# Loads of the norm weights on another queue, and the first q and k transposes of the second batch in another PSUM bank

## The chip, the cores and the metric

The kernel runs on one core of a Trainium2 chip. Five engines work from instruction streams of their own[...]: TensorE (PE, matmuls and their weight loads, PEld), VectorE (DVE), ScalarE (ACT), GpSimd (POOL) and SyncE (SP, which here only issues DMAs). The metric is the device time of one execution in microseconds (us); lower is better.

## The reference

Two stages follow each other. The first is attention over 8 batches, 12 heads, 448 positions and a head size of 64, with q and k normalised by their root mean square:

```python
q_n = q / sqrt(mean(q*q) + 1e-6) * g_q          # the same for k with g_k
scores = softmax(q_n @ k_n.T / sqrt(64))
attn = scores @ v
```

The second takes the heads side by side as x (3584 rows, 768 columns) and applies `h = x @ w_in` (2048 columns), `g = h * clip(h + 3, 0, 6) / 6`, `out = g @ w_out`. Inputs and output are float32 in HBM.

## The kernel before, in words

**Tiling.** The unit of attention is a pair of heads, P = 0 to 47, six pairs to a batch. A pair passes through five functions:

- `loads` brings k, q and v of the pair in three DMAs of 224 KB. All are issued by SP, except that q of the first three pairs is issued by ACT. Buffers for k and q are five deep.
- `prep` squares q and k (line 320 on ACT for the first three pairs, lines 322 and 329 on DVE or POOL for the others), sums the squares per head and row (DVE, line 337), turns the sums into 1/rms (two ACT instructions, lines 343 and 344), multiplies (line 351, `qks`, DVE or POOL), and casts v (POOL, line 359, `va`).
- `turn` transposes k and q so that the head size lies on the partitions. For P below `NPE` = 10, that is the whole first batch (P 0 to 5) and four pairs of the second (P 6 to 9), PE does it: eight transposes of 112x112 (line 377) into one PSUM bank, then two copies by DVE out of the bank, `kp` (line 381, multiplied by `gp`) and `kq` (line 383). From P = 10 on a DMA transpose does it (line 388), and `kp` is made by POOL or DVE (line 392).
- `attend` makes the scores (PE, line 416, into the two-bank buffers S) and their exponentials (ACT, line 421), four tiles to a pair.
- `gather` multiplies by v (PE, line 437) into the bank X (positions 0 to 383) and the bank R (the last 64), and DVE normalises out of X (lines 462 and 463, `xn`). For the first batch PE transposes `xn` into an M bank (line 476) and DVE copies it to `xT` (line 480); later batches use DMA transposes (line 486).

`gp`, one value per partition, is 8 * g_q * g_k. It is made once by DVE (line 270) from four loads of 64 values each (`load_g`, lines 254 and 255): g_q and g_k, each once for the upper and once for the lower 64 partitions.

The MLP of a batch follows one batch later: `h_group` (line 533, six matmuls into an M bank, then ACT line 539 and DVE line 541 out of it) sixteen times, and `y_group` (line 558, sixteen matmuls into an M bank, then DVE line 566). Its matmuls are spread between the attention of the next batch. The weights w_in and w_out come through eight DMAs of POOL's queue (lines 277 and 283), held back by a small copy on POOL (line 621, `mark`) until q of the third pair has landed.

**PSUM.** There are eight banks: two S buffers of two banks each, X with one, R with one, and M with two. Each is a `Ring`: a taker waits until everyone who used the buffer before it is done. In the kernel before, the M ring serves `turn` (P 0 to 9), the `xn` transposes of the first batch, `h_group` and `y_group`, in the order in which these are called. X serves `gather` alone.

**Order.** Each piece of work is a `Step` with the engines that may take it, an expected duration, a due time and the steps it depends on. `Plan.order` is a list scheduler over these: it walks through time, gives each engine the ready step that is due first, and so fixes the order on every engine and, where a step may go to DVE or POOL, the engine. The program then issues in that order; on the chip each engine keeps to it. A changed duration, engine or dependency can therefore reorder work anywhere behind it. The loads of SP and ACT take eight completion semaphores in turn, and a load waits on its own queue until the earlier load with the same semaphore has landed. The loads of POOL have eight of their own.

Of the kernel before, what the change touches and what calls it, by code (L numbers as in the profile page):

```python
# [33 lines left out]
class Plan:  # L34
# [12 lines left out]
    def add(self, on, dur, due, fn, *deps, xfer=0.0, after=0.0, lock=False, late=0.0):  # L47
        on, f = ({on: dur}, lambda e: fn()) if isinstance(on, str) else (on, fn)
        s = Step(on, due, f, deps, xfer, after, lock, late, len(self.steps))
        self.steps.append(s)  # L50
        return s
# [93 lines left out]
def kernel(  # L145
# [11 lines left out]
    nc = tc.nc  # L157
# [3 lines left out]
    NJ = H // 2  # L161
# [14 lines left out]
    def tiles(name, n, shape, dt=BF16, pool=const):  # L176
        return [pool.tile(shape, dt, name=f"{name}{i}") for i in range(n)]

    gq_t, gk_t, gp = (const.tile([128, 1], FP32, name=n) for n in ("gq_t", "gk_t", "gp"))
# [23 lines left out]
    X_r = Ring(tiles("X", 1, [128, 512], FP32, psum))  # L203
    R_r = Ring(tiles("R", 1, [128, 512], FP32, psum))
    M_r = Ring(tiles("M", 2, [128, 512], FP32, psum))

    plan = Plan()
    add = plan.add
# [42 lines left out]

    def load_g():
        for a in range(2):
            nc.scalar.dma_start(out=gq_t[a * 64:(a + 1) * 64, :], in_=g_q.rearrange("(p o) -> p o", o=1))
            nc.scalar.dma_start(out=gk_t[a * 64:(a + 1) * 64, :], in_=g_k.rearrange("(p o) -> p o", o=1))

    def make_ident():
        nc.gpsimd.memset(ident[:], 0.0)
# [4 lines left out]
    def make_ones():  # L263
        for t in va_r.bufs:
            nc.gpsimd.memset(t[:, :, :, D:E1], 1.0)
        for t in kp_r.bufs:
            nc.gpsimd.memset(t[:, S:S + 16], 0.0)

    g_load = add("ACT", 2.2, 0, load_g, after=1.5, late=3.0)
    g_make = add("DVE", 0.1, 0, lambda: nc.vector.scalar_tensor_tensor(  # L270
        out=gp[:], in0=gq_t[:], scalar=8.0, in1=gk_t[:], op0=MULT, op1=MULT), g_load, after=7.5)
    id_make = add("POOL", 0.5, 0, make_ident)
# [92 lines left out]
    def turn(P):  # L365
        at = begin[P]
        qks, qks_use, sc, va, va_use, vc = SC.pop(P)
        kq, war, kq_use = kq_r.take()
        kp, kwar, kp_use = kp_r.take()
        if P < NPE:  # L370
            m, mwar, m_use = M_r.take()
            pt = m[:].bitcast(BF16)[:, 0:2 * S].rearrange("p (i c) -> p i c", i=2)
            tr = []
            for i in range(2):
                def trans(i=i):
                    for t in range(T):
                        nc.tensor.transpose(  # L377
                            out=pt[:, i, t * PT:(t + 1) * PT],
                            in_=qks[0:PT, i, t].rearrange("p h d -> p (h d)"), identity=ident[0:PT, 0:PT])
                tr.append(add("PE", 0.4, at - 2, trans, sc[i], id_make, *mwar))  # L380
            ks = add("DVE", 0.45, at - 1, lambda: nc.vector.tensor_scalar_mul(  # L381
                kp[:, 0:S], pt[:, 0], gp[:, 0:1]), tr[0], g_make, one_make, *kwar)
            qc = add("DVE", 0.45, at - 1, lambda: nc.vector.tensor_copy(out=kq[:, 1], in_=pt[:, 1]), tr[1], *war)
            m_use += [ks, qc]
            qks_use += tr
            KQ[P] = (kq, kp, va, kq_use, kp_use, va_use, [ks, qc], vc)
        else:
            tr = add("SP", 1.3, at - 8, lambda: nc.sync.dma_start_transpose(
                out=kq[:].rearrange("p i (t c) -> p (i t) c", c=PT),
                in_=qks[0:PT].rearrange("p i t h d -> p (i t h d)")), *sc, *war, xfer=1.3, late=1.5)  # L390
            ks = add({"DVE": 0.34, "POOL": 0.6}, 0, at - 1, lambda e: (
                nc.vector if e == "DVE" else nc.gpsimd).tensor_scalar_mul(  # L392
                    kp[:, 0:S], kq[:, 0], gp[:, 0:1]), tr, g_make, one_make, *kwar, lock=True)
            qks_use.append(tr)
            kq_use.append(ks)
            KQ[P] = (kq, kp, va, kq_use, kp_use, va_use, [ks], vc)
# [232 lines left out]
    for P in range(NP):  # L629
        for fn, at in ((loads, -26), (prep, -13), (turn, -2), (attend, 0)):  # L630
            blocks.append((begin[P] + at, lambda fn=fn, P=P: fn(P)))
        blocks.append((begin[P + 1] + 0.1, lambda P=P: gather(P)))
# [41 lines left out]
```

## Time and profile before

| what | us |
|---|---|
| median of 4 runs | 441.49 (440.89 to 443.41) |
| the profiled execution, its own time | 440.89 |
| its span, first to last instruction | 439.1 |
| PE busy in the span | 410.4 |
| DVE, ACT, POOL busy | 245.0, 249.0, 240.5 |

The span is 1.8 us shorter than the time of the same execution. PE busy counts the stretches in which at least one matmul is in flight. Lines with a q after the engine (ACTq, SPq) are its sequencer, which issues DMAs and waits. The release named behind an idle stretch is the semaphore that came last. The clock that TensorE was granted is full in every slice.

### The profile page before, as it was taken

To read this page: it belongs to the slowest core of one execution; us is meant where nothing else is said; L and a number is where in the kernel's file an instruction comes from. 1 tells how busy PE (TensorE), PEld (TensorE's weight loads), DVE (VectorE), ACT (ScalarE), POOL (GpSimd) and SP (SyncE) were. 2 spreads that over 40 slices of the span, in tenths; PEclk is the share of its full clock that TensorE was granted. 3 is DMA by queue.
4 is the path that set the end of the run, shared out by engine and by line. 5 is a ranking of instruction groups with operands and counts; after the bars stand their busy time and mean duration, and the time that the engine had idled before them with its cause. 6 is when DMAs were issued, how large, how long until landed. Compare 5 with 4: busy or idle time off the path is not lost.

```text
span 439.1 us, 9205 instructions
## 1 busy us (share of the span) xinstructions
PE 410.4 (93%) x3663; PEld 229.1 (52%) x3682; DVE 245.0 (56%) x417; ACT 249.0 (57%) x425; POOL 240.5 (55%) x230
## 2 busy tenths in 40 slices
PE   0598799999999999999999999999999999999995
PEld 0255455555455555554455555554455555654563
DVE  1998887557674564456455465556564444334421
ACT  2688588657765666367664677357673665123200
POOL 3499988865757567656765657747757510000000
PEclk9999999999999999999999999999999999999999
DMA  9999999897455646674466655684466420220122
GB/s 232 258 269 261 221 216 196 206 185 204 113 136 141 186 116 138 162 214 116 128 156 163 171 138 149 159 210 113 116 162 168 97 56 11 64 72 0 37 72 73
DMA packets 102923, 64.58 MB, mean 147 GB/s; under 512 B 59744, under 2 KB 99424, under 8 KB 102880
## 3 DMA queue, kind: packets, MB, share of 16 engines
q1 hardware_dynamic: 94544, 57.01, 51.1%
q0 software_dynamic: 7296, 6.29, 9.2%
q10 hardware_dynamic: 1040, 0.69, 0.6%
q8 instruction: 29, 0.48, 0.4%
q14 instruction: 14, 0.11, 0.1%
HBM read 45.61 MB, written 11.01 MB: 129 GB/s over the span
## 4 chain that ended last, share of the span: by engine, by line
PE 82%; POOL 5%; DVE 3%; DMA 3%; issue 3%; ACT 2%; SPq 1%; POOLq 0%; DVEq 0%
PE M L558 27%; PE M L533 26%; PE S L416 9%; PE X L437 8%; PE S L558 4%; PE R L437 2%; PE S L533 2%; DMA qk<-in_k_dram 1%; POOL qks L351 1%; PE X L558 1%; DVE ssq L337 1%; POOL va L359 1%; POOL sq L322 1%; ACT e L421 1%; POOL sq L329 1%
## 5 line engine op out<-in xcount | busy, mean ns | idle before, releaser
L421 ACT ACTIVATE e<-S 112x896 bf16<-112x896 f32 x192 | 166.4, 914 | 64.1 <-PE S L416 64.1
L533 PE MATMUL M<-xT,w_in_sb 128*128 128x384 bf16 (+1 forms) x679 | 145.1, 349 | 3.8 <-DVE gT L541 3.0
L351 POOL TENSOR_TENSOR qks<-qk,rs 112x512 bf16<-112x512 f32 x87 | 90.6, 1057 | 85.9 <-ACT rs L344 84.0
L558 PE MATMUL M<-w_out_sb,gT 128*128 128x384 bf16 x736 | 131.8, 326 | 0.0
L558 PEld LDWEIGHTS <-gT 128*128 128x128 bf16 x896 | 82.9, 98 | 57.9 <-issue 7.8
L533 PEld LDWEIGHTS <-w_in_sb 128*128 128x128 bf16 x768 | 69.6, 97 | 67.5 <-issue 12.6
L541 DVE SCALAR_TENSOR_TENSOR gT<-t,M 128x384 bf16<-128x384 f32 (+1 forms) x116 | 70.7, 612 | 59.2 <-ACT t L539 58.5
L539 ACT ACTIVATE t<-M 128x384 f32<-128x384 f32 (+1 forms) x116 | 62.7, 540 | 66.8 <-PE M L533 65.3
L437 PEld LDWEIGHTS <-e 112*128 112x128 bf16 x1536 | 65.0, 99 | 31.4 <-issue 16.0
L337 DVE TENSOR_REDUCE ssq<-sq 112x16 f32<-112x1024 f32 (+1 forms) x49 | 58.4, 1193 | 25.3 <-POOL sq L329 14.0
L329 POOL TENSOR_TENSOR sq<-qk 112x1024 f32<-112x1024 f32 x36 | 68.3, 1896 | 0.0
L416 PE MATMUL S<-kq,kp 64*128 64x448 bf16 x384 | 56.6, 364 | 4.0 <-DVE kp L381 1.7
L437 PE MATMUL X<-va,e 112*128 112x65 bf16 x1152 | 58.5, 195 | 0.8 <-ACT e L421 0.6
L566 DVE COPY y<-M 128x384 f32<-128x384 f32 x46 | 25.6, 556 | 59.4 <-PE M L558 59.2
L359 POOL CAST va<-vf 112x512 bf16<-112x512 f32 x48 | 31.5, 658 | 10.2 <-DMA vf<-in_v_dram 9.3
L392 POOL TENSOR_SCALAR kp<-kq,gp 128x448 bf16<-128x448 bf16 x23 | 32.3, 1405 | 5.8 <-DMA kq<-qks 5.8
L463 DVE TENSOR_TENSOR xn<-X,rd 128x384 bf16<-128x384 f32 x48 | 26.8, 558 | 1.6
L416 PEld LDWEIGHTS <-kp 64*128 64x128 bf16 x384 | 12.2, 94 | 27.6 <-issue 18.8
L377 PE MATMUL M<-ident,qks 112*128 112x112 bf16 x80 | 8.0, 242 | 13.6 <-DVE qks L351 13.0
L437 PE MATMUL R<-va,e 112*128 112x65 bf16 x384 | 20.4, 195 | 0.0
L558 PE MATMUL S<-w_out_sb,gT 128*128 128x384 bf16 x112 | 19.5, 326 | 0.0
L462 DVE RECIPROCAL rd<-X 128x6 f32<-128x6 f32 x48 | 9.2, 192 | 14.7 <-PE X L437 14.6
(42 smaller groups left out, 155.0 us busy)
## 6 DMA issues: line engine op xcount, KB each, us to landing
qk<-in_k_dram SPq DMA_DIRECT2D x48, 224.0 KB, 3.2
vf<-in_v_dram SPq DMA_DIRECT2D x48, 224.0 KB, 3.9
qk<-in_q_dram SPq DMA_DIRECT2D x45, 224.0 KB, 3.5
w_in_sb<-in_moe_w_in_dram POOLq DMA_DIRECT2D x4, 768.0 KB, 10.4
w_out_sb<-in_moe_w_out_dram POOLq DMA_DIRECT2D x4, 768.0 KB, 10.7
out_dram<-y SPq DMA_DIRECT2D x8, 336.0 KB, 3.1
out_dram<-y SPq DMA_DIRECT2D x8, 288.0 KB, 3.6
out_dram<-y SPq DMA_DIRECT2D x8, 240.0 KB, 3.5
```

Source lines behind the costliest of these rows:

```text
L329: parts = [add("POOL", 1.93, at - 10, lambda: nc.gpsimd.tensor_tensor(out=sq[0:PT], in0=qk[0:PT], in1=qk[0:PT], op=MULT), *ld, *war, lock= ...
L337: red = add("DVE", 0.6 * n, at - 8 * hurry + 0.5 * i0, lambda i0=i0, i1=i1, cs=cs: nc.vector.tensor_reduce(out=ssq[0:PT, cs], in_=sq[0:PT, ...
L351: sc.append(add(on, 0, at - 6 * hurry, lambda e, i=i, rs4=rs4: engines[e].tensor_tensor(out=qks[0:PT, i].rearrange("p t h d -> p h t d"), ...
L359: vc = add({"POOL": 0.61}, 0, at - 3, lambda e: engines[e].tensor_copy(out=va[0:PT, :, :, 0:D], in_=vf[0:PT].rearrange("p h (t d) -> p h t ...
L392: nc.vector if e == "DVE" else nc.gpsimd).tensor_scalar_mul(
L416: nc.tensor.matmul(out=ps[:, a, 0:S], lhsT=kp[rows, c0:c0 + 128], rhs=kq[rows, 1, :], start=True, stop=True)
L421: x = add("ACT", 0.93, at + step * (t0 + i) / T + 0.2, lambda t=t0 + i, ps=ps: nc.scalar.activation(out=e[0:PT, t], in_=ps[0:PT, :, 0:S], ...
L437: nc.tensor.matmul(out=dst[:, a * E1:(a + 1) * E1], lhsT=e[0:PT, t, a, c0:c0 + 128], rhs=va[0:PT, a, t, :], start=(first and a == 0 and t ...
L533: nc.tensor.matmul(out=m[:, 0:n], lhsT=w_in_sb[:, kt, f * 128:(f + 1) * 128], rhs=X[:, kt, :], start=(kt == 0), stop=(kt == NKT - 1))
L539: r = add("ACT", 0.08 + n / 1200, due + span, lambda: nc.scalar.activation(out=t[:, 0:n], in_=m[:, 0:n], func=RELU, bias=0.5, scale=1.0 / ...
L541: g = add("DVE", 0.12 + n / 960, due + span, lambda: nc.vector.scalar_tensor_tensor(out=G[:, f, :], in0=t[:, 0:n], scalar=1.0, in1=m[:, 0: ...
L558: nc.tensor.matmul(out=m[:, 0:HALF], lhsT=G[:, f, i * 128:(i + 1) * 128], rhs=w_out_sb[:, f, cols], start=(f == 0), stop=(f == NFT - 1))
```

## The change

Two edits. The four loads of `load_g` are issued by POOL and no longer by ACT, with another entry for the planner: 2.5 on POOL, due at 1, in place of 2.2 on ACT, due at 0 and not before 1.5. And `turn` takes its bank from the M ring only for the first batch (`NJ` = 6); for P 6 to 9 it takes X.

```diff
     def load_g():
         for a in range(2):
-            nc.scalar.dma_start(out=gq_t[a * 64:(a + 1) * 64, :], in_=g_q.rearrange("(p o) -> p o", o=1))
-            nc.scalar.dma_start(out=gk_t[a * 64:(a + 1) * 64, :], in_=g_k.rearrange("(p o) -> p o", o=1))
+            nc.gpsimd.dma_start(out=gq_t[a * 64:(a + 1) * 64, :], in_=g_q.rearrange("(p o) -> p o", o=1))
+            nc.gpsimd.dma_start(out=gk_t[a * 64:(a + 1) * 64, :], in_=g_k.rearrange("(p o) -> p o", o=1))
...
-    g_load = add("ACT", 2.2, 0, load_g, after=1.5, late=3.0)
+    g_load = add("POOL", 2.5, 1, load_g, late=3.0)
...
         if P < NPE:
-            m, mwar, m_use = M_r.take()
+            m, mwar, m_use = (M_r if P < NJ else X_r).take()
```

In the order that results, POOL issues the four loads after its memsets and before `mark`; on DVE `gp` stands behind both `qks` of the first pair; five squares more go to DVE and five fewer to POOL, three `qks` go from DVE to POOL, and two `kp` of the later pairs go from POOL to DVE.

## The prediction

> **What bounds the kernel now.** I read the busy table first, then the sums by stage, then the order of time at the start, the chain, and PE's order of time where the second batch begins. From the page:
>
> ```profile
> span 439.1 us, 9205 instructions
> PE 410.4 (93%) x3663; PEld 229.1 (52%) x3682; DVE 245.0 (56%) x417; ACT 249.0 (57%) x425; POOL 240.5 (55%) x230
> ```
>
> PE is idle for 28.7 us of the span. Where that lies is in the sums by stretch (busy time of PE, PEld, DVE, ACT, POOL, then clock, DMA share and GB/s):
>
> ```profile
> 0.00:9.00 9.00, 0.00 (x0) 0.00 (x0) 0.00 (x0) 1.30 (x2) 2.26 (x17) 1.00 0.86 227
> 9.00:15.00 6.00, 1.35 (x10) 0.86 (x12) 4.81 (x9) 4.34 (x12) 1.97 (x3) 1.00 1.14 227
> 15.00:25.00 10.00, 7.78 (x67) 3.99 (x63) 9.96 (x13) 7.02 (x12) 6.78 (x8) 1.00 1.16 271
> ...
> 35.00:46.00 11.00, 8.43 (x125) 5.15 (x125) 9.77 (x20) 8.61 (x15) 10.99 (x12) 1.00 1.16 260
> 46.00:60.00 14.00, 11.99 (x136) 7.66 (x135) 11.85 (x20) 9.52 (x21) 13.46 (x16) 1.00 1.23 216
> 60.00:75.00 15.00, 14.85 (x150) 8.17 (x148) 11.37 (x23) 12.96 (x24) 13.67 (x12) 1.00 1.14 194
> 75.00:376.00 301.00, 298.84 (x2709) 165.27 (x2724) 167.40 (x284) 186.72 (x314) 182.17 (x158) 1.00 0.57 145
> ```
>
> From 75 us on PE is the bound: 2.2 us idle in 301. Whatever brings PE sooner to that stage, with the same work done, comes off the end. Before it there are three stages: a start without PE work (to about 12 us), the first batch (to 46), where DVE and then POOL are nearly full, and the first MLP groups (to 60), where PE stalls for 2 us. In the order of time the start reads:
>
> ```profile
> 4.18 0.53 ACTq L254 DMA_DIRECT2D gq_t<-in_g_q_dram  x1
> 4.75 0.60 ACTq L255 DMA_DIRECT2D gk_t<-in_g_k_dram  x1
> ...
> 7.12 0.47 ACTq L254 DMA_DIRECT2D gq_t<-in_g_q_dram  x1
> ...
> 8.47 0.47 ACTq L255 DMA_DIRECT2D gk_t<-in_g_k_dram  x1
> 8.99 1.67 ACT L320 ACTIVATE sq<-qk 112x512 f32<-112x512 f32 x3 [6.98 <-DMA gq_t<-in_g_q_dram]
> ...
> 12.16 0.16 DVE L270 SCALAR_TENSOR_TENSOR gp<-gq_t,gk_t 128x1 f32<-128x1 f32 x1 [0.44 <-DMA gk_t<-in_g_k_dram]
> ```
>
> The first square starts at 8.99, though its data are there long before: the first k load is issued at 0.73 and takes 3.4 us to land (4.16), the first q 3.8 from 0.76 (4.55). ACT does not come to it, because each of its four g loads waits for an earlier load with the same completion semaphore: they go out when the first k, the first q, v of pair 0 and k of pair 2 have landed. The squares stand behind. The chain confirms it: it is the longest piece of the first 12 us, followed by a g load that holds DVE until 12.16.
>
> ```profile
> 2.17 6.28 DMA qk<-in_k_dram
> 8.47 3.56 DMA gk_t<-in_g_k_dram
> ```
>
> Where the second batch begins, PE's order of time shows the M banks (line 533 is an MLP group, 377 a turn):
>
> ```profile
> 45.99 2.12 PE L533 MATMUL M<-xT,w_in_sb 128*128 128x384 bf16 x12
> ...
> 49.68 1.14 PE L533 MATMUL M<-xT,w_in_sb 128*128 128x384 bf16 x6 [0.53 <-DVE gT L541]
> 50.65 0.56 PE L377 MATMUL M<-ident,qks 112*128 112x112 bf16 x8
> 52.21 1.14 PE L533 MATMUL M<-xT,w_in_sb 128*128 128x384 bf16 x6 [1.00 <-DVE gT L541]
> ```
>
> The turn takes the second M bank, so two MLP groups follow each other in one bank, and the second waits 1.00 us until DVE has emptied it. With a third wait of 0.47 at 56.85, PE waits 2.0 us there for line 541.
>
> [...] ACT is idle for 6.98 us with its data landed. [...] The gain here isn't bandwidth but the place in ACT's queue. [...]
>
> **The change part by part.**
>
> *ACT without the g loads.* The first square (q is first in the new order) starts at 4.57 in place of 8.99: 4.42 us. The pieces behind it: before, the two 1/rms values end at 11.42, 2.43 after the first square's start. In the new order a square of pair 1's q (landed 5.95, 0.61 long) precedes the first of them, so they run from 6.58, four at some 0.2 with gaps, to 7.44. DVE's two `qks` (0.69 each) end at about 8.4, `gp` takes 0.16, the reduction for pair 1 1.2, and `kp` starts at about 9.7 in place of 13.97. Start: 4.3 us earlier.
>
> *POOL with the g loads.* POOL is idle from 1.6 to 7.75. The nearest row is the issue of w_in, 0.89 to 1.05 each with far more rows; four such are 4.2 us, done by 5.9 and covered by that idle time. [...] Landing: ACT's g loads took 3.6 to 5.5 us[...]. [...] DVE comes to `gp` at 8.4, so the cost is 0 to 3.0; I take 0, since on POOL's queue the g loads stand behind nothing, while on ACT's they stood behind three 224 KB loads. Nothing else waits for them: `mark` waits for a q load until 7.7 anyway, and w_in goes out 0.5 us sooner.
>
> *The first batch behind it.* DVE has no idle time to speak of from 12 to 46 us. To the last `xT` copy the new order gives it three squares more (2.1), four `qks` fewer (2.8) and one reduction earlier (1.2): 0.5 later. POOL loses most of its idle 4.0 and 3.2 us (at 14.1 and 21.9) and runs ahead, so it stops being the limit. The DMA engines are full (share above 1), so loads don't come sooner by the whole 4.3 us. From pair 4 on DVE and POOL reached the data 0.7 to 14 us after landing. Closest is q of pair 4, landed at 16.86; the new order wants it on DVE at about 16 to 17. Cost 0 to 1.0, I take 0.5.
>
> *Turns in X.* Pair 6 is at the seam. Its turn must now wait until DVE has normalised pair 4 out of X, and pair 5's `gather` until both copies of pair 6 are out. After the end of pair 4's matmuls that is 0.75 (normalise), 0.69 (a square ahead on DVE; the turn's 0.56 runs beside it), 0.82 (copies) and five hand-overs of 0.15 to 0.2: 3.1 us. Those matmuls end some 1.5 us after ACT begins with pair 5, whose four exponentials of 0.92 last to 3.7; the scores of pair 6 come at 4.6. Cost about 0.9, bounds 0 to 1.5. For pairs 7 to 9 the same round trip has some 7 us of MLP and attention work per pair around it; X is asked for once as a turn and once as a gather, and in the new order MLP groups stand on PE between them. I take 0; uncovered, the price stands under the rivals.
>
> *M without turns.* The 1.00 us wait goes, since groups alternate between banks again. The other two (0.53, 0.47) come from DVE's lateness and half remains. I take 1.5 of the 2.0; bounds 0 and 2.0.
>
> *Behind 75 us.* The last 120 runs of PE's order are the same; the 2.2 us of idle time can shift by 0.5 either way.
>
> Sum: -4.3 + 0.5 + 0.5 + 0.9 - 1.5 = -3.9 us. Against the profiled execution's 440.89 (the span and 1.8 around it) that is 437.0; its time is 0.6 below the median, so the median goes from 441.49 to 437.6.
>
> **Rivals.**
>
> *Supply takes it back.* DMA engines or a late `gp` hold the first batch: 1.0 us at pair 4, some more at pair 6 (landed 25.5, wanted about 25), or 3.0 at `gp`. For it: a DMA share of 1.14 to 1.16. Against it: a DMA held line 270 by 0.44 us only, and from there to 60 us the waits show no compute instruction held by one. Gain 1 to 3, about 1.8: 439.7.
>
> *Nothing comes of it.* The first batch is paced by DVE and the order behind it, and the saved start turns up as idle time before the first MLP group. Speaks for it: DVE at 9.96 of 10. Against: DVE's own work also starts 4.3 us sooner. About 441.5.
>
> *More than forecast.* DVE finds its data, `gp` is early, all of the 2.0 and part of the 1.52 us that PE waits for `xn` at 45.23 go: 6 to 7 us, about 435.
>
> *X becomes the bound (slower).* Each turn of P 6 to 9 sits in PE's order before other work and stops it for the round trip through DVE. With nothing to cover it 0.75 + 0.56 + 0.82 and four hand-overs are 2.8 us, four times 11. It decides from 1.2 us a turn on: the other parts gain 4.3 - 0.5 - 0.5 + 1.5 = 4.8 us, over four. Against it: X is free for most of a pair's 7 us in the second batch. At 2 us each: 8.0 - 4.8 = 3.2 more than before, 444.7.
>
> **How the numbers follow.** A measurement of this kernel tells about 0.5%, 2.2 us, from no change. Forecast (gain 3 to 6): 0.50, all faster. More than forecast: 0.07, faster. Supply: 0.25, of which 0.09 faster and 0.16 same. Nothing: 0.07, same. X: 0.11, of which 0.09 slower and 0.02 same. Faster 0.66, same 0.25, slower 0.09. The range 434.8 to 441.9 leaves out the best of the gains and the slower case, some 0.15 together; the forecast's own range is 435.5 to 438.5.
>
> **What would show it.** ACT's first square at about 4.6, idle before it until a qk load lands and not a g load; `gp` before 9; `kp` at 9.7; the first scores near 10.5; the first group of line 533 near 43.6; no waits of 1 us for line 541 between two groups in one bank. Wrong: line 270 held by a DMA for over 1 us; POOL or DVE waiting for qk loads between 15 and 30; PE idle before line 377 or 437 on X for more than 1 us a pair from pair 6 on; a first MLP group no sooner than 45.

## The result, and the profile after

The changed kernel takes 443.95 us (median of 43 runs, 441.9 to 448.93), the kernel before 441.6 beside it (64 runs): a ratio of 1.0061 with a 95% interval of 1.0047 to 1.0076. It is 0.6% slower, where the prediction had it 0.9% faster and its range ended at 441.9. The profiled execution took 441.90, the fastest of them, against 440.89 before; so the traces show 1.0 us of the 2.35 between the medians. All medians here count every run, and the ratios leave out runs more than 1.5% above the fastest of their kernel.

From the page of the changed kernel:

```profile
span 440.1 us, 9197 instructions
PE 412.9 (94%) x3664; PEld 229.0 (52%) x3682; DVE 243.8 (55%) x421; ACT 250.3 (57%) x425; POOL 237.9 (54%) x230
```

PE is idle for 27.2 us in place of 28.7, but busy for 2.5 us more with the same work. So time was lost in two ways: the early start was given back as waits, and some matmuls ran slower. The sums by stretch (PE, PEld, DVE, ACT, POOL, then granted clock, DMA share, GB/s) say where:

```profile
0.00:9.00 9.00, 1.11 (x8) 0.64 (x8) 2.57 (x4) 4.94 (x11) 4.25 (x20) 1.00 0.69 204
9.00:15.00 6.00, 2.39 (x14) 0.97 (x15) 4.93 (x7) 3.27 (x8) 4.73 (x7) 1.00 1.08 274
...
25.00:35.00 10.00, 8.15 (x104) 5.13 (x104) 8.72 (x18) 7.55 (x13) 8.77 (x11) 0.83 1.18 245
...
46.00:60.00 14.00, 12.46 (x105) 6.58 (x105) 10.76 (x19) 8.40 (x16) 10.92 (x12) 0.88 1.26 231
60.00:75.00 15.00, 14.78 (x163) 8.32 (x163) 12.30 (x24) 12.95 (x25) 13.09 (x12) 1.00 1.14 199
75.00:376.00 301.00, 297.06 (x2694) 163.46 (x2710) 164.66 (x285) 186.08 (x312) 178.44 (x155) 1.00 0.60 145
```

The two values under 1.00 in the clock column are stretches at half clock, from 30.8 and from 47.9 us; the execution of the kernel before that was profiled has none of them. Most of its other runs had some: only 65 of the 204 beside these experiments reach a mean granted clock of 0.998. And the long stretch has 3.94 us of PE idle time in place of 2.16. Followed through the traces, the lead of the changed kernel is:

| point | before, us | after, us | lead |
|---|---|---|---|
| first square (line 320) | 8.99 | 4.55 | 4.44 |
| `gp` (line 270) | 12.16 | 10.06 | 2.10 |
| first scores (line 416) | 14.76 | 12.06 | 2.70 |
| first MLP group (line 533) | 45.99 | 42.56 | 3.43 |
| first matmul of line 558 | 74.71 | 72.90 | 1.81 |
| 241st matmul of line 558 | 181.8 | 180.1 | 1.74 |
| 289th | 206.7 | 206.3 | 0.39 |
| 481st | 284.4 | 285.2 | -0.80 |
| span | 439.1 | 440.1 | -1.0 |

Three places matter. **The start**, POOL's and DVE's order of time:

```profile
1.67 0.75 POOL L254 DMA_DIRECT2D gq_t<-in_g_q_dram  x1
...
3.46 0.55 POOL L255 DMA_DIRECT2D gk_t<-in_g_k_dram  x1
```

```profile
7.05 1.29 DVE L351 TENSOR_TENSOR qks<-qk,rs 112x512 bf16<-112x512 f32 x2 [0.57 <-ACT rs L344]
10.06 0.16 DVE L270 SCALAR_TENSOR_TENSOR gp<-gq_t,gk_t 128x1 f32<-128x1 f32 x1 [1.72 <-DMA gk_t<-in_g_k_dram]
```

The issues are cheap, 2.4 us in all under POOL's idle time. But the four loads landed at 7.28, 8.35, 9.31 and 9.93, 5.6 to 6.5 us after their issue, and DVE waited 1.72 us for the last. Of the 4.44 us of lead 2.70 are left at the first scores. In the first batch it grows again, to 3.43: PE's wait for `xn` ahead of the first MLP group falls from 1.52 to 0.63 us, and PE reaches full speed sooner. The clock column hides the second: the record of the clock begins at 26.1 us before and at 20.6 after, and the column reads 1.00 up to there. But pairs of matmuls of line 416 took 0.55 us up to 25.2 us in the kernel before and 0.36 from 26.7 on, and the same step comes at 20 to 21 us in the changed one.

**The first MLP groups**, PE's and DVE's order of time:

```profile
42.56 2.12 PE L533 MATMUL M<-xT,w_in_sb 128*128 128x384 bf16 x12
44.51 0.36 PE L377 MATMUL X<-ident,qks 112*128 112x112 bf16 x4
44.71 0.42 PE L437 MATMUL R<-va,e 112*128 112x65 bf16 x8
47.52 3.68 PE L533 MATMUL M<-xT,w_in_sb 128*128 128x384 bf16 x12 [2.38 <-DVE gT L541]
```

```profile
42.78 0.45 DVE L381 TENSOR_SCALAR kp<-X,gp 128x448 bf16<-128x448 bf16 x1
43.15 0.68 DVE L351 TENSOR_TENSOR qks<-qk,rs 112x512 bf16<-112x512 f32 x1
43.75 1.10 DVE L322 TENSOR_TENSOR sq<-qk 112x512 f32<-112x512 f32 x1
45.78 1.22 DVE L337 TENSOR_REDUCE ssq<-sq 112x16 f32<-112x1024 f32 x1 [0.93 <-POOL sq L322]
46.92 1.01 DVE L541 SCALAR_TENSOR_TENSOR gT<-t,M 128x384 bf16<-128x384 f32 x2
```

The turn of pair 7 no longer sits in an M bank, as meant, and groups 0 and 1 follow each other at once. Then both M banks are full, and DVE empties them only at 46.92: in the new order `kp` of pair 7, pair 8's `qks`, pair 9's square and pair 9's reduction stand ahead, the last with a wait for POOL's half of the square. PE idles 2.38 us where it idled 0.53, and the next twelve matmuls take 3.68 us in place of 2.12. The old order had something ahead of the first `gT` too. DVE's order of time before:

```profile
46.42 1.22 DVE L337 TENSOR_REDUCE ssq<-sq 112x16 f32<-112x1024 f32 x1
47.94 1.22 DVE L337 TENSOR_REDUCE ssq<-sq 112x16 f32<-112x1024 f32 x1 [0.31 <-POOL sq L322]
49.08 1.01 DVE L541 SCALAR_TENSOR_TENSOR gT<-t,M 128x384 bf16<-128x384 f32 x2
```

Between the last copy to `xT` and the first `gT` DVE took 3.05 us before (46.03 to 49.08) and 4.52 after (42.40 to 46.92). Counted from the first MLP group, `gT` comes 1.27 us later, and PE had 0.59 us less of other work to fill the time; together that is the 1.85 us by which the wait grew.

The half clock lies in whole stretches of 3.4 us, whose bounds stand on one grid through a trace. On that grid, two stretches of the changed kernel with the one that follows each, and one of the kernel before, which was followed by full clock:

```profile
27.40:30.82 3.42, 1.79 (x25) 1.08 (x24) 3.27 (x8) 2.11 (x5) 2.96 (x5) 1.00 1.17 245
30.82:34.24 3.42, 3.42 (x41) 2.19 (x37) 2.29 (x5) 2.69 (x5) 2.65 (x5) 0.50 1.18 245
44.47:47.88 3.41, 1.02 (x17) 0.75 (x15) 2.48 (x5) 0.93 (x3) 3.17 (x3) 1.00 1.23 254
47.88:51.30 3.42, 3.42 (x13) 1.42 (x13) 1.50 (x4) 0.56 (x2) 2.67 (x4) 0.50 1.12 289
```

```profile
43.18:46.59 3.41, 1.89 (x27) 1.09 (x25) 3.25 (x7) 2.17 (x3) 3.41 (x4) 1.00 1.22 259
```

TensorE was granted half its clock for 3.4 us after a stretch in which it worked 1.02 of 3.41 us. How much work went ahead of half clock doesn't come out as one number: it followed 1.79 us in the changed kernel, and full clock followed 1.89 us in the kernel before; in e4 half clock followed 2.27 us and full clock 1.56. Over all traces here, from the start of each record of the clock, every stretch at full clock with less than 1.5 us of work was followed by half clock (13 of 13), none with more than 2.28 was, and in between both came. What sets it is not shown.

**Behind 75 us**, PE waits for `gT` at 109.5 (0.61), 200.7 (1.18), 217.4 (0.42) and 275.2 (0.43). The largest, in POOL's and then DVE's order of time:

```profile
192.99 0.61 POOL L359 CAST va<-vf 112x512 bf16<-112x512 f32 x1 [7.11 <-DMA vf<-in_v_dram]
...
195.96 1.04 POOL L351 TENSOR_TENSOR qks<-qk,rs 112x512 bf16<-112x512 f32 x1
196.96 1.89 POOL L329 TENSOR_TENSOR sq<-qk 112x1024 f32<-112x1024 f32 x1
```

```profile
198.88 1.22 DVE L337 TENSOR_REDUCE ssq<-sq 112x16 f32<-112x1024 f32 x1 [1.33 <-POOL sq L329]
200.02 1.27 DVE L541 SCALAR_TENSOR_TENSOR gT<-t,M 128x512 bf16<-128x512 f32 x2
```

POOL waits for a load of v, whose cast stands in its order ahead of the square, the reduction on DVE waits for the square, and `gT` stands behind the reduction. The same place in POOL's order of time before:

```profile
188.97 2.04 POOL L351 TENSOR_TENSOR qks<-qk,rs 112x512 bf16<-112x512 f32 x2 [1.96 <-ACT rs L344]
192.41 0.61 POOL L359 CAST va<-vf 112x512 bf16<-112x512 f32 x1 [1.40 <-DMA vf<-in_v_dram]
192.98 1.90 POOL L329 TENSOR_TENSOR sq<-qk 112x1024 f32<-112x1024 f32 x1
```

This v landed at 192.87, hardly later than before (192.29). But before, two `qks` stood ahead of its cast and were done in the time; in the new order they and a `kp` stand behind it, so POOL idles from 185.9 on and the square ends at 198.85 in place of 194.88. In the mean over pairs 14 to 46 v lands 1.3 us later than before, and POOL comes to its cast 1.4 us sooner: the place of the cast counts as much as the landing. The groups of line 359 of the page, after and before, show that the wait is new: 42.9 us of POOL's time wait for v in place of 9.3.

```profile
L359 POOL CAST va<-vf 112x512 bf16<-112x512 f32 x48 | 30.4, 636 | 60.7 <-DMA vf<-in_v_dram 42.9
```

```profile
L359 POOL CAST va<-vf 112x512 bf16<-112x512 f32 x48 | 31.5, 658 | 10.2 <-DMA vf<-in_v_dram 9.3
```

### The profile page after: what moved, and what is told of

Same layout as the page of the kernel before. It is cut to its first block, busy times and chain, and to the rows that moved or that the text cites. A ratio compares the mean times of both kernels' runs of the same rounds, so it can differ in the third digit from the quotient of the medians.

```text
span 440.1 us, 9197 instructions
## 1 busy us (share of the span) xinstructions
PE 412.9 (94%) x3664; PEld 229.0 (52%) x3682; DVE 243.8 (55%) x421; ACT 250.3 (57%) x425; POOL 237.9 (54%) x230
## 4 chain that ended last, share of the span: by engine, by line
PE 70%; DMA 10%; POOL 7%; DVE 6%; SPq 3%; issue 2%; ACT 1%; POOLq 0%; another core or an unknown queue 0%
PE M L558 24%; PE M L533 20%; DMA vf<-in_v_dram 8%; PE S L416 7%; PE X L437 7%; PE S L558 4%; POOL qks L351 3%; DMA qk<-in_k_dram 2%; PE S L533 2%; POOL sq L329 2%; DVE ssq L337 2%; PE R L437 2%; DVE gT L541 1%; POOL kp L392 1%; PE X L558 1%
## 5 line engine op out<-in xcount | busy, mean ns | idle before, releaser
L533 PE MATMUL M<-xT,w_in_sb 128*128 128x384 bf16 (+1 forms) x680 | 149.2, 352 | 5.7 <-DVE gT L541 4.8
L351 POOL TENSOR_TENSOR qks<-qk,rs 112x512 bf16<-112x512 f32 x90 | 93.6, 1055 | 45.5 <-ACT rs L344 42.0
L437 PEld LDWEIGHTS <-e 112*128 112x128 bf16 x1536 | 66.6, 99 | 33.8 <-issue 17.2
L359 POOL CAST va<-vf 112x512 bf16<-112x512 f32 x48 | 30.4, 636 | 60.7 <-DMA vf<-in_v_dram 42.9
L437 PE MATMUL X<-va,e 112*128 112x65 bf16 x1152 | 59.9, 196 | 0.5 <-ACT e L421 0.5
L392 POOL TENSOR_SCALAR kp<-kq,gp 128x448 bf16<-128x448 bf16 x21 | 29.5, 1405 | 4.5 <-DMA kq<-qks 4.5
L343 ACT ACTIVATE rs<-ssq 112x16 f32<-112x16 f32 (+1 forms) x49 | 10.7, 218 | 15.9 <-DVE ssq L337 15.7
L392 DVE TENSOR_SCALAR kp<-kq,gp 128x448 bf16<-128x448 bf16 x17 | 13.9, 819 | 3.8 <-DMA kq<-qks 3.8
```

The costliest lines, as they stand in the source:

```text
L351: sc.append(add(on, 0, at - 6 * hurry, lambda e, i=i, rs4=rs4: engines[e].tensor_tensor(out=qks[0:PT, i].rearrange("p t h d -> p h t d"), ...
L359: vc = add({"POOL": 0.61}, 0, at - 3, lambda e: engines[e].tensor_copy(out=va[0:PT, :, :, 0:D], in_=vf[0:PT].rearrange("p h (t d) -> p h t ...
L437: nc.tensor.matmul(out=dst[:, a * E1:(a + 1) * E1], lhsT=e[0:PT, t, a, c0:c0 + 128], rhs=va[0:PT, a, t, :], start=(first and a == 0 and t ...
L533: nc.tensor.matmul(out=m[:, 0:n], lhsT=w_in_sb[:, kt, f * 128:(f + 1) * 128], rhs=X[:, kt, :], start=(kt == 0), stop=(kt == NKT - 1))
```

## The experiments

Theory "order": what costs is not the edits but the order that the planner made of them. Theory "supply": the weight stream holds the DMA engines until 70 us, and a lead before that is lost to it. Ratios are to the kernel before, run beside it. e4 has one run, e5 four, e8 five and e7 eight.

| run | kernel | median, us | ratio [95%] |
|---|---|---|---|
| e1 | g edit alone, re-planned | 443.92 | 1.0028 [1.0005, 1.0052] |
| e2 | X edit alone, re-planned | 446.08 | 1.0082 [1.0062, 1.0103] |
| e3 | g edit, order of before | 442.07 | 0.9990 [0.9974, 1.0005] |
| e4 | after, light w_in | 443.04 | - |
| e5 | after, `gT` first | 448.25 | 1.0145 [1.0097, 1.0192] |
| e6 | after, v early | 442.92 | 1.0009 [0.9974, 1.0043] |
| e7 | e3, w_out late | 445.60 | 1.0072 [1.0042, 1.0102] |
| e8 | before, w_out late | 447.65 | 1.0108 [1.0070, 1.0146] |
| e9 | before, light weights | 444.67 | 1.0051 [1.0032, 1.0070] |
| e10 | e3, light weights | 444.29 | 1.0047 [1.0027, 1.0067] |
| e11 | after, light weights | 442.02 | 0.9992 [0.9964, 1.0020] |
| e12 | after, `gp` without g | 443.92 | 1.0043 [1.0020, 1.0067] |
| e13 | before, v early | 441.89 | 1.0003 [0.9984, 1.0022] |
| e14 | e3, v early | 441.76 | 0.9994 [0.9974, 1.0014] |
| e15 | e1, v early | 442.38 | 1.0011 [0.9990, 1.0032] |
| e16 | after, v early, `gT` first | 442.57 | 1.0010 [0.9981, 1.0038] |
| e17 | e14, g loads first | 443.43 | 1.0012 [0.9991, 1.0032] |

### Each edit alone (e1, e2)

e1 is the changed kernel with

```diff
-            m, mwar, m_use = (M_r if P < NJ else X_r).take()
+            m, mwar, m_use = M_r.take()
```

> The g loads on GpSimd's queue with the new entry for the planner, all turns in the M banks as before. Theory S (supply): what costs time in the changed kernel is that GpSimd runs ahead after the early start and sends the weight loads sooner, so that v of pair 9 lands at 43.5 us and not 38 and holds GpSimd, then DVE, then PE; that comes from the g edit alone, so here too v of pair 9 lands after 42, PE waits over 1.5 us for line 541 near 45, and the time is within 1.5 us of before (440 to 443). Theory X (the turns in X cost it): without them the early start is kept, first MLP group at 43 and first group of line 558 before 72, time 437 to 439.

e2 is the kernel before with the opposite line, g still on ScalarE.

> The turns of pairs 6 to 9 in X, the g loads on ACT's queue as before. Theory X: the time rises by 2 to 5 us (444 to 447), with PE waits before lines 377, 437 or 416 on X's round trip from 40 to 65 us. Theory S: the start is that of before, the weight loads go out within 1 us of before, no load is late, the M banks are free: 439.5 to 441.5. Theory R (the order behind the first batch, made anew by the planner, is worse whichever edit made it): PE waits for line 541 after 100 us come to over 1.5 us in total here too, and the time is 441.5 to 444.

Both are slower than the kernel before, e1 by little. In e1 the first MLP group comes at 43.11, 2.9 us early, and is followed by nine waits of line 533 for `gT`, 7.8 us in all. In e2 nothing starts early, and the seam costs more than the 0.9 us that the prediction gave pair 6: the first MLP group comes at 47.44, 1.45 us later than before. PE's order of time in e2:

```profile
41.11 0.55 PE L377 MATMUL X<-ident,qks 112*128 112x112 bf16 x8 [1.59 <-DVE xn L463]
...
43.16 0.93 PE L416 MATMUL S<-kq,kp 64*128 64x448 bf16 x4 [1.06 <-DVE kq L383]
```

The turn of pair 6 waits 1.59 us until pair 4 is out of X, the scores another 1.06 for the copies. At 51.40 a wait of 2.27 for `xT` follows, and 10 us at half clock around it. All its 18 runs have a mean clock of 0.986 to 0.988. Since each edit comes with an order of its own, e1 and e2 don't price the edits by themselves.

### The order kept (e3)

The loads of g go to GpSimd, but the planner is told of the kernel before, so every engine keeps its old order.

```diff
-            nc.scalar.dma_start(out=gq_t[...], in_=g_q...)
+            nc.gpsimd.dma_start(out=gq_t[...], in_=g_q...)
...
     g_load = add("ACT", 2.2, 0, load_g, after=1.5, late=3.0)
```

> The four g loads are issued by GpSimd after its memsets, but the planner is told of before's ACT step, so every engine keeps the order of before; turns stay in M. The early start without the new order. All theories: first square at 4.6, gp near 10, first scores near 12 as in the changed kernel. Theory R: PE behind 75 us waits no more than before (1 us), and the 2.7 us of the start arrive at the end: 438 to 439.5. Theory S: the loads cannot follow, GpSimd and DVE wait for k, q and v between 15 and 45 us, and under 1.5 us arrive: 440 to 441.5.

The same time as before, where 438 to 439.5 or 440 to 441.5 was expected. The lead is 2.17 us at every step until 68 us, with the same three waits of 0.53, 1.00 and 0.47 for `gT`. Then, in PE's order of time and by stretch:

```profile
71.76 0.93 PE L416 MATMUL S<-kq,kp 64*128 64x448 bf16 x4 [2.23 <-POOL kp L392]
```

```profile
68.00:71.70 3.70, 1.53 (x10) 0.69 (x8) 1.37 (x2) 2.10 (x6) 1.41 (x2) 1.00 1.32 193
71.70:75.10 3.40, 3.34 (x26) 1.78 (x27) 1.05 (x3) 1.73 (x2) 3.40 (x4) 0.50 1.09 217
```

The DMA transpose of pair 10's kq, issued at 58.85, landed at 70.20, with the last part of w_out (70.22). Before, it landed at 69.38, issued 2.2 us later. The lead is lost to a transfer that didn't move, and 3.4 us at half clock follow the idle time. So the old order is not a cure either: it has a lead, and the late transfer takes it at pair 10.

### The weights out of the way (e4, e9 to e11)

e4 loads and uses a sixth of w_in; e9 to e11 also an eighth of w_out:

```diff
-            out=w_in_sb[:, :, c * n:(c + 1) * n],
-            in_=moe_w_in[:, c * n:(c + 1) * n]...
+            out=w_in_sb[:, 0:1, c * n:(c + 1) * n],
+            in_=moe_w_in[0:128, c * n:(c + 1) * n]...
...
-            out=w_out_sb[:, f0:f0 + NFT // 2, cols],
+            out=w_out_sb[:, f0:f0 + 1, cols],
```

> The changed kernel, but only the first sixth of w_in is loaded and used in place of all six (the output is therefore another): the four w_in loads shrink from 768 to 128 KB each, and no instruction moves. Theory S: v of pair 9 lands before 38 us, GpSimd's wait before its cast goes, PE's wait for line 541 near 45 falls from 2.4 to under 0.7 us and the half clock from 48 to 51 us goes; first group of line 558 about 4 us sooner than in the changed kernel (69 and not 72.9). Theory X or R: the wait of over 2 us stays, and that group comes within 1 us of 72.9.

A single run, 443.04. v of pair 9 lands at 29.1 in place of 43.5, and the third group still waits:

```profile
48.89 2.11 PE L533 MATMUL M<-xT,w_in_sb 128*128 128x384 bf16 x12 [1.85 <-DVE gT L541]
```

With DVE's steps in this order the third group waited 2.38 us in the changed kernel, 1.85 here, 2.32 in e11, 2.59 in e12 and 1.14 in e6. So the order comes with at least 1.1 us, in place of the 0.53 of the old one; the rest moves with POOL's half of the square and with how long DVE's multiplications take, and the single run doesn't divide it.

> The kernel before with light weights: of w_in only the first 128 rows are loaded and used for all six steps, of w_out only the first 128 rows of each loaded part, so 12.6 MB become 1.8 MB; the instructions and their order stay, the output differs. Control for e10 and e11. Both theories: the first line 558 within 1.5 us of 74.7 (in the kernel before PE waits for nothing that the weights hold up), median 440 to 442.

> As e9, with the loads of g on GpSimd and the order of the kernel before (e3 with light weights). Theory 'supply' (the lead of e3 is lost because the transposed kq of pair 10 lands behind the weights): kq of pair 10 lands within 5 us of its issue, no wait at 71.8, and the median is 1.7 to 2.5 us under e9. Rival 'something else at pair 10' (POOL's or SP's own order): a wait of 1 us or more stays between 65 and 76, and the median is within 0.8 us of e9.

> As e9, for the changed kernel. Theory 'supply' as the whole cause: with the weights out of the way the changed kernel keeps its early start and is 2 to 3.5 us under e9, and POOL waits for v less than 15 us. Theory 'order as well' (the new order of DVE and POOL costs by itself: f2 waits behind the square and reduction of pair 9, and gT behind reductions later): the wait of f2 stays over 1.5 us, gT waits behind 75 us stay over 2 us together, and the median is within 1 us of e9 or above it.

The control moved by itself: e9 is 0.5% slower than the kernel before with its weights, against both theories. The trace shows where, in DVE's order of time of e9, then in DVE's and POOL's of e10:

```profile
40.88 3.22 DVE L351 TENSOR_TENSOR qks<-qk,rs 112x512 bf16<-112x512 f32 x2 [0.19 <-ACT rs L344]
```

```profile
40.22 4.70 DVE L351 TENSOR_TENSOR qks<-qk,rs 112x512 bf16<-112x512 f32 x2 [0.19 <-ACT rs L344]
```

```profile
40.61 1.03 POOL L322 TENSOR_TENSOR sq<-qk 112x512 f32<-112x512 f32 x1
...
43.20 1.16 POOL L359 CAST va<-vf 112x512 bf16<-112x512 f32 x2
```

Two `qks` that take 0.68 to 0.69 us each where POOL is idle (at 11.03 and 12.24 in the kernel before) take 3.22 us together in e9 and 4.70 in e10, 2.14 in the kernel before at this place. POOL's squares and casts lie beside them, in the kernel before too (squares from 42.34, a cast from 43.88). Why the `qks` take longer in e9 and e10 isn't shown; POOL waited for no load at this place in the kernel before either. The two `qks` are the last DVE work ahead of `xT`, and PE waits for `xn` behind them for 1.52 us before, 2.60 in e9 and 4.08 in e10 (at 45.67). So e10 is level with e9 (0.4 us of medians, within the noise) and didn't test supply: the wait at pair 10 is gone as expected (none over 0.25 us between 59 and 175), while the lead had been lost before, at 45 us.

e11 answers its own question. Its first line 558 comes at 71.42, 4.6 us ahead of e9, although the third group still waits 2.32 us; POOL still waits 43.7 us for v, and behind 75 us PE waits 3.0 us, 2.11 of it at 200.5 with 3.4 us at half clock after it. In the profiled executions nothing of the 4.6 us is left at the end; over all runs e11 is 2.65 us under e9, as "supply" had it. But e9 is held up by its `qks`, so the fairer comparison is the changed kernel with and without its weights, 1.0061 and 0.9992. Both theories are met in part: the weights do hold the changed kernel up, and the waits for `gT` belong to its order, with or without them.

### The third group's wait, and late v (e5, e6, e13 to e16)

e5 moves pair 9's square and reduction, and the ACT step behind them, after the first two `gT` in the issue order (the steps are collected where they are made):

```diff
+        steps = plan.order()
+        for x in late9[:3]:
+            steps.remove(x)
+        k = steps.index(late9[3]) + 1
+        steps[k:k] = late9[:3]
```

> The changed kernel, but in the issue order the square and the reduction of pair 9 on DVE (and the two ACT steps behind the reduction) come after the first two gT of the MLP (line 541) and no longer before them; nothing else moves. Theory 'order' (the new order of DVE holds the M banks, PE idles 2.4 us and then runs 3.4 us at half clock): the wait of f2 for gT falls from 2.38 to under 0.8 us, no half clock at 48 to 51 us, the first matmul of line 558 comes about 2.4 + 1.7 us earlier than 72.9, at 69 to 70, and the median is 2 to 4 us under the changed kernel's 444.0. Rival 'supply' (the weight stream fills the DMA engines until about 70 us, and transposed kq of pairs 11 and 12 lands at 71 to 73 whatever PE does): the wait goes, but PE then waits for kp of a DMA-transposed pair before 72, line 558 starts at 72 to 73, and the median stays within 1 us of 444.0.

The wait goes, as "order" expected; the time rises to 448.25, which neither theory expected. The trace is that of the slowest of the four runs (451.3; the others took 447.9 to 448.3). PE's, DVE's, POOL's and SP's order of time:

```profile
76.28 2.08 PE L533 MATMUL M<-xT,w_in_sb 128*128 128x384 bf16 x6 [5.68 <-DVE gT L541]
```

```profile
74.55 1.22 DVE L337 TENSOR_REDUCE ssq<-sq 112x16 f32<-112x1024 f32 x1 [6.24 <-POOL sq L329]
```

```profile
72.62 1.89 POOL L329 TENSOR_TENSOR sq<-qk 112x1024 f32<-112x1024 f32 x1 [1.50 <-DMA qk<-in_q_dram]
```

```profile
59.76 0.44 SPq L302 DMA_DIRECT2D qk<-in_q_dram  x1
...
63.42 6.74 SPq L388 DMA_TRANSPOSE kq<-qks  x1
```

POOL's square waits for a q load that was issued at 59.76 and landed at 72.46, 12.7 us later. In the changed kernel the same load took 7.7 us, from 58.87 to 66.61. SP's stand of 6.74 us at a transpose (2.02 in the changed kernel) comes behind this load and doesn't hold it. From 60 to 65 us the DMA engines were busier than in the changed kernel (share 1.50 in place of 1.26) and moved less (103 GB/s in place of 201). So in this execution it is "supply": a load that had been issued and was slow to land. Why so little was moved there isn't shown.

e6 issues v of a pair right behind its q, from pair 8 on:

```diff
+        for P, q_load, v_load in pairs[8:]:
+            steps.remove(v_load)
+            steps.insert(steps.index(q_load) + 1, v_load)
```

> The changed kernel, but from pair 8 on SP issues the load of v right behind the load of q of the same pair, ahead of what stood between them (DMA transposes and stores). Theory 'late v' (v lands late, so the cast on POOL holds POOL, POOL's square comes late, DVE's reduction waits for it and gT behind it): POOL's wait for v at line 359 falls from 42.9 us to about 10, the four PE waits for gT behind 75 us (109, 200, 217, 275 us, 2.6 us together) fall below 1 us, and the median falls by 1.5 to 3 us against 444.0. Rival 'order alone' (DVE has its reductions ahead of gT there in any case): the v waits fall, the PE waits stay above 2 us, and the median stays within 1 us of 444.0.

POOL's wait for v falls from 42.9 to 15.8 us and PE's waits for `gT` behind 75 us from 2.6 to 0.4 in one place. The cast that waited longest still waits, but it is done 2.3 us sooner, and the reduction and `gT` behind it follow without a wait:

```profile
190.70 0.61 POOL L359 CAST va<-vf 112x512 bf16<-112x512 f32 x1 [6.42 <-DMA vf<-in_v_dram]
```

```profile
197.06 1.21 DVE L337 TENSOR_REDUCE ssq<-sq 112x16 f32<-112x1024 f32 x1
198.19 0.68 DVE L541 SCALAR_TENSOR_TENSOR gT<-t,M 128x512 bf16<-128x512 f32 x1
```

The median falls by 1.0 us, and the ratio from 1.0061 to 1.0009, each to the kernel before run beside it; the two intervals just miss each other. Its twelve runs scatter from 439.83 to 446.17, six of them under 442 and six over 444, and the trace is one of the first six. e13 and e14 are the controls, with the same shift in the old order; e15 leaves the X bank out; e16 joins e5 and e6.

> The kernel before with the same shift of the v loads as in e6: from pair 8 on SP issues v right behind q of the same pair. Control: POOL waits only 9.3 us for v in the kernel before, and PE 0.7 us for gT behind 75 us. If late v is what the new order added, this stays within 1 us of the kernel before (441 to 443). If earlier v loads are a gain in any order, it is 1 us or more faster, and e6 says nothing on the change.

> The loads of g on GpSimd in the order of the kernel before (e3), and v right behind q as in e6. In e3 the lead of 2.2 us was lost at 71.8 us to kq of pair 10, which an earlier v does not relieve. Expected: within 1 us of e3's 442.1. If it falls below 441, late v was part of e3's loss as well.

> The changed kernel without its second edit (e1: turns of pairs 6 to 9 in the M banks), with v right behind q as in e6. Beside e6 it tells what the X bank is worth once late v is out of the way. If the X bank helps by itself (no M bank is taken by turns while the first MLP groups run), this is 1 us or more slower than e6's 442.9. If the order is all that differs, it is within 1 us of it.

> The changed kernel with both shifts: v right behind q (e6), and square and reduction of pair 9 behind the first two gT (e5). If the two causes add up and nothing else holds PE, the wait of f2 (2.38 us, and 3.4 us of half clock after it) and the gT waits behind 75 us are both gone: 439 to 441, faster than both kernels. If, as in e5, PE then only meets the weight stream sooner, there is a wait of 3 us or more between 68 and 78 us and the time is 444 or more.

Earlier v does nothing in the old order (e13 is level with the kernel before, e14 within 0.3 us of e3), so late v is one thing that the new order added. e15 against e6 finds no worth and no cost of the X bank, 1.0011 and 1.0009; but their orders differ in more than the bank, and these runs resolve no less than some 1.4 us. In e16 both waits are gone (none for `gT` ahead of the third group or behind 75 us is over 0.25 us), but 1.41 us at 49.2 (copies of pair 7), 0.76 at 50.9 and 1.63 at 73.2 have come. It took 442.57 and not 439 to 441: of fourteen runs seven lie between 439.7 and 441.8 and seven between 443.3 and 449.5. They go with the granted clock (0.990 to 1.000 in the first seven, 0.978 to 0.992 in the others), which the two halves of e6 don't; what sends an execution to the one or the other isn't settled.

### The weights later (e7, e8), and the landing of g (e12, e17)

e7 and e8 issue the last two w_out loads behind the transposes of pair 11:

```diff
+        for x in (W_out[2], W_out[3]):
+            steps.remove(x)
+        k = steps.index(turned[1]) + 1
+        steps[k:k] = [W_out[2], W_out[3]]
```

> The loads of g on GpSimd with everything else in the order of the kernel before (as in e3), and the last two loads of w_out (its right half, first read by the fourth group of line 558) issued only after the DMA transposes of kq of pairs 10 and 11. Theory 'supply' (in e3 the lead of 2.2 us was lost because kq of pair 10 landed 11 us after its issue, behind the weights): kq of pair 10 lands before 66, the wait of 2.23 us at 71.8 and the half clock after it go, line 558 starts at about 72.5 (2.2 before the kernel before), and the median is 439.5 to 440.5, about 2 us under the kernel before. Rival: the lead is lost at another place (the fourth group of line 558 waits for w_out, or xT of batch 1), and the median is 441.5 to 443.

> The kernel before with the same shift of the last two w_out loads, and g still on ScalarE: the control for e7. If the gain of e7 is the early start, this one stays within 0.7 us of the kernel before (442), because PE has no wait for kq of pair 10 there. If the shift of w_out is what helps by itself, it is as fast as e7.

A failed remedy. In e7 the wait for pair 10 falls to 0.29 us, but POOL reached the two loads at 63 to 64 us, beside pair 11's transpose. In e8 DVE waits 2.63 us for pair 11's transpose, at 74.31. It moved the wait by one pair, and the shift alone costs 5 us (e8). With the same shift e7's median is 2 us under e8's, but the runs are few, the intervals overlap, and in the profiles its first MLP group leads by 0.7 us only.

e12 sets `gp` without waiting for g:

```diff
-    g_make = add("DVE", 0.1, 0, lambda: nc.vector.scalar_tensor_tensor(
-        out=gp[:], in0=gq_t[:], scalar=8.0, in1=gk_t[:], op0=MULT, op1=MULT), g_load, after=7.5)
+    g_make = add("DVE", 0.1, 0, lambda:
+        nc.vector.memset(gp[:], 8.0), g_load, after=7.5)
```

> The changed kernel, but gp is set to 8.0 by a memset on DVE at the same place in its order; the four loads are still issued, and nobody waits for them (g_q and g_k are left out of the result). It measures what the landing of g costs by itself. My forecast took 0: then the first scores stay at about 12. If the landing is what holds gp (1.7 us of waiting for gk in the changed kernel's profile), the first scores come 1.5 to 2 us earlier, near 10.3, as the forecast's sum had it. For the end: theory 'supply' says that this lead too is gone by 75 us, median within 1 us of 444.0; the rival, that a start earlier by 1.7 us reaches the end, says 442.3.

PE's order of time:

```profile
10.30 0.93 PE L416 MATMUL S<-kq,kp 64*128 64x448 bf16 x4 [1.24 <-DVE kq L383]
14.33 0.55 PE L377 MATMUL M<-ident,qks 112*128 112x112 bf16 x4 [3.10 <-POOL qks L351]
```

The first scores come at 10.30, 1.76 us sooner, as the forecast's sum had it. But the turn of pair 1 comes at 14.33 (13.54 in the changed kernel), since its loads and `qks` are no sooner, and the median doesn't move. The landing of g was a real wait; what it costs the end is within what these runs resolve, some 0.8 us.

e17 is e14 with the step `g_load` issued first of all (`steps.remove(g_load); steps.insert(0, g_load)`).

> e14 (loads of g on GpSimd, order of the kernel before, v right behind q) with the four loads of g issued by GpSimd ahead of its memsets, about 0.9 us earlier. Theory 'landing' (gp waits for the last of the four loads, which lands 7 to 8 us after its issue): gp at about 10.5 to 10.8 in place of 11.66, the first scores at 13.3 or a little before, against 14.76 in the kernel before; if this lead reaches the end, the median is 440.5 to 441.2 and this version beats both kernels. Rival: the landing is set by the other loads that fill the DMA engines, gp stays at 11 or later, or the lead is gone by 76 us as in e3, and the median stays within 0.5 us of 441.8.

The loads go out 0.4 us sooner and not 0.9, and the last lands at 10.59, against 11.53 in e14; over all profiles with g on GpSimd it landed between 9.82 and 11.53. `gp` comes at 10.72; a wait of 1.95 us for pair 10's kq at 73.55 takes the lead, as in e3. No version ran measurably faster than the kernel before.

## Why the prediction was wrong

- **ACT without the g loads** was right: first square at 4.55, predicted 4.57. One reading on the way was too large: ACT was not idle for 6.98 us "with its data landed". The first k and q landed at 4.16 and 4.55, so only some 4.4 us of the 6.98 lie behind the landing, and these are the gain.
- **POOL with the g loads.** The issue was right (2.4 us, covered). "I take 0" for the landing was wrong: 1.72 us, inside the bounds of 0 to 3.0. Of these the upper one is an estimate from the trace before (the last issue done by 5.9, 5.5 us to land as at the most on ACT, DVE there at 8.4); the lower one was the author's estimate alone. The argument failed that on POOL's queue they "stand behind nothing". They were under way beside the first k, q and v loads (DMA share 0.69 up to 9 us, 1.08 behind). The prediction allowed for a share above 1 with the large loads and not with these. That this is what made them late was not shown: no run tested it. The prediction's own sign of being wrong, line 270 held for over 1 us, came. e12 shows that the term doesn't decide the end.
- **The first batch, with the turn of pair 6**, came out near the sum by luck: first group predicted at 43.6, measured at 42.56, out of two errors that cancel. The start gained 2.70 us at the first scores and not 4.3, and from there to the first group the lead was to fall by 1.9 us and grew by 0.7. At pair 6 the scores wait 0.68 us for the copies out of X, forecast 0.9. The hand-overs of 0.15 to 0.2 us in that sum were the author's estimate and are not what the trace shows there: 0.04 us from the turn to `kp` (38.41 to 38.45) and 0.06 from `kq` to the scores (39.20 to 39.26). The turns of pairs 7 to 9 cost nothing visible, as forecast: from 42 to 75 us no wait of PE on X is over 0.25 us.
- **"M without turns", 1.5 us of gain**, is a step that failed. The wait between groups in one bank went, but in its place came 2.38 us for the same `gT`, and some 1.6 us at half clock (3.68 in place of 2.12). From the first group to the first matmul of line 558 the lead was to grow by 1.5 us; it fell by 1.6. The prediction counted how much work DVE has up to `xT`, and not what stands on DVE between `xT` and the first `gT`. That is in the order that could be read beforehand: a `qks`, a square and a reduction, 3.0 us, where two reductions stood before, 2.4. e5 shows that the wait goes when the order is changed; e4 and e6 show that its size also moves with POOL's half of the square.
- **"Behind 75 us", shifts of 0.5**, is the other: a lead of 1.81 became a lag of 0.80, 2.6 us. The prediction looked at the last 120 runs of PE's order. They are the same only from 309 us on; the loss lies between 181 and 285 us, where PE's order differs in some places too, and of the 2.6 us 1.9 are idle time and 0.7 busy time. What the prediction didn't look at is POOL's order, where casts of v moved ahead of the `qks` that used to fill the time until v lands, and hold up the squares. PE waits 2.6 us for `gT` behind 75 us in the changed kernel, 0.4 with v early (e6), 1.0 in the kernel before and 0.2 in e13.
- **The sum.** The forecast was -3.9 us, the traces show +1.0. The 4.9 between them are 1.6 at the start, -2.6 in the first batch, 3.1 at "M without turns" and 2.8 behind 75 us (to the end of the span).
- **The half clock** has no term in the sum. The mean granted clock was 0.991 over the runs of the changed kernel and 0.996 to 0.997 over those of the kernel before; over 440 us that is an estimated 2 to 3 us at the most, if PE was busy throughout. Over the runs of the kernel before, those at 0.985 to 0.993 are 2.4 us slower than those at 0.998 and up. But in the runs of the changed kernel clock and time hardly go together (447.16 us at 0.999), and e6 has 0.991 too and lost less. How much of the loss is half clock was not isolated.
- **The rivals.** "Supply takes it back" named the right resource at the wrong place: not pair 4 or 6, but pair 10's transpose at 70 us (e3, e17) and, in e5, a q load that took 12.7 us. Its "Against" read the waits for DMAs up to 60 us only; behind that, POOL waited 3.3 us for pair 10's transpose in the kernel before already. It put the result between no gain and the forecast, and had no term for the order. "X becomes the bound" fell.

What is shown: each edit as planned is slower; earlier v takes back part of the loss in the new order (1.0 us of medians, 2.3 by the ratios, with wide intervals) and nothing in the old one; the third group's wait goes with DVE's order. What stays open: the new order without either edit was not run, nor the X bank in the old order; why POOL comes to the casts sooner; why e6 and e16 scatter over 6 to 10 us; and how what is left divides between half clock and supply.

## What to carry to other kernels

A lead at the start is worth what survives the next shared limit: follow it through the weight stream, the first DMA transposes and the first full banks before it is booked. Where a planner orders the work, compare the orders of every engine and of the DMA queues to the end, and read what stands directly ahead of the instruction that frees a bank, and what stands behind one that waits for a load; a sum of work per engine doesn't tell it. Idle time of PE is priced with the half clock that may follow it (here 3.4 us of it after a wait of 2.38). And a sum that comes out right is checked term by term, since errors cancel, as in the first batch here.

## What the runs showed of the hardware

- Half clock came in whole stretches of 3.4 us (3.4, 6.8 and 10.2 us), on one grid in each trace, after stretches in which PE had worked up to 2.28 us of 3.41, and not only after empty ones. Under 1.5 us of work it always came. Twelve matmuls took 3.68 us at half clock and 2.12 at full; from these two, a stretch adds an estimated 1.6 us to the wait before it.
- The record of the clock began 20.6 to 26.1 us into the two main traces and reads 1.00 up to there, while pairs of score matmuls took 0.55 us that later took 0.36.
- The 65 runs of the kernel before with a mean granted clock of 0.998 and up had a median of 441.02 us, the 112 from 0.993 to 0.998 one of 442.60, the 27 from 0.985 to 0.993 one of 443.46.
- A load of 64 values of 4 bytes from GpSimd took 5.2 to 8.1 us from issue to landing beside the first large loads, and the four landed 0.5 to 2.3 us apart.
- DMA transposes of kq issued while weights were on the way landed after 10 to 11.4 us in e3 and 5.7 to 8.2 in the changed kernel; at the same place with light weights after 2.6 to 3.3 us (e9, e11).
- Two DVE multiplications of 0.69 us stretched to 2.14, 3.22 and 4.70 us together beside POOL's squares and casts (the kernel before, e9, e10).
